# The second product of a mixture-of-experts kernel with its weights stationary, and row blocks turned on VectorE

## The chip, the cores and the metric

One of the eight cores of a Trainium2 chip runs the whole program. The metric is the time of one execution on the device in microseconds (us). TensorE (PE in the profile) multiplies: a weight load (PEld) puts a stationary operand of up to 128x128 into the array, and a matmul streams the columns of the moving operand past it into a bank of PSUM. VectorE is DVE, ScalarE is ACT, GpSimd is POOL and issues the indirect DMAs, SyncE (SP) issues the others.

## The reference, cut to what matters

Three layers follow one another: an attention between 512 tokens and 32 state rows per head, a dense layer with two products, and a mixture of eight experts.

```python
# attention: x [8, 8, 512, 64], state [8, 8, 32, 64]; rows read from the state, and state rows read from x
xread = softmax(x @ state.T / 8) @ state
sread = softmax(state @ x.T / 8) @ x
x = concat([xread, sread], axis=2)            # -> 4352 tokens x 512 after the heads are put side by side

# dense layer: w_in [512, 2048], w_out [2048, 512]
h = x @ w_in
g = h * clip(h + 3, 0, 6) / 6
x = g @ w_out                                  # the second product

# experts: w1 [8, 512, 1024], w2 [8, 1024, 512]
logits = x @ w_gate
e = argmax(logits)
gate = softmax(logits)[e] * sigmoid(x @ w_output_gate)[e]
out = gate * (relu(x @ w1[e]) @ w2[e])
```

## The kernel before

All products with high accuracy are made of three matmuls in the fp32r type: an operand is split into a high part (`gh`, `woh`, `sh`, `ah`) and a rest (`gl`, `wol`, `sl`, `al`), and high x high, high x rest and rest x high are added in one bank.

The dense layer is worked through in batches of 512 tokens (b = 0 to 7), and at the end the 256 state tokens (b = NB). A batch has 16 slices ft of the hidden dimension. For each, `h_xread` (state tokens: `h_sread`) makes a bank h of 128 hidden values by all tokens, `act` makes g, gh and gl from it on ACT and DVE in four instructions, and two slices later (LAG = 2) `second` calls `gemm2` for it. `gemm2` takes one token tile of 128 after another: gh and gl of the tile are stationary, the slice of w_out moves, and the bank `po[t]` collects 128 tokens by 512 model values over the 16 slices. The batches go in the order 0 (first half of the slices), 1, 0 (second half), 2 to 7, state tokens; the half results of batch 0 are kept in DRAM meanwhile (`half0`) and come back as `part`.

When a batch is through, `routed` scales its four banks by 1/6 into four row tiles `xr` of 513 values (ACT and DVE in turn; batch 0 on DVE, which adds `part`). During the next batch a timetable by slice number does the rest: steps 2 and 3 turn the rows (`turn_rows`: four TensorE transposes for a token tile into a bank, then a DVE copy to x2T), steps 6 to 8 multiply by the gate weights (`logits`, `turn_logits`), steps 9 to 11 choose the expert (`choose`), count the places (`ranks`) and, in `place`, make the gate weight, write it behind the row as its 513th value, and send the row tile to `xd` in DRAM; `scatter` writes the token numbers to a table `tab` at the tokens' places. A run of such TensorE instructions stays together (`one_run`) and waits before its first one for all that it needs. Batch 1 has a shorter timetable (`half_timetable`), batch 7 and the state tokens are routed between other instructions (`route`, `at_will`).

The experts are then run in slots of 256 places: `gather` reads token numbers out of `tab` and with them rows out of `xd`; `turn` turns the rows with TensorE and copies the gate weight out of the 513th value with POOL; `gemm1` and `gemm2e` are the products; `finish` scales by the gate and scatters rows to the output.

SP issues its DMAs in the order of the program: loads of the next batch (xT at step 2, xq at step 3), row writes at step 11. A tile's tag names a ring of buffers of which `bufs` exist; a writer waits until an earlier user of the buffer is done. The row tiles have the tag "xr" with four buffers of 2 KB; x2T lies in "x2T" (one) and for the second half of a batch in the ring "x4" of the loaded inputs.

Of the kernel before, what the change touches and what calls it, by code (L numbers as in the profile page):

```python
# [26 lines left out]
ROW = DM + 1  # L27
# [20 lines left out]
def cat_consts():  # L48
# [25 lines left out]
    tok = np.zeros((128, NT // 128), np.uint32)  # L74
    tok[:] = np.arange(NT).reshape(-1, 128).T
    fill = (NT + np.arange(NTAB).reshape(-1, 2) % 128).astype(np.uint32)
# [4 lines left out]
def tile_kernel(  # L81
# [32 lines left out]

    xd = tc.dram_tile([NT + 128, ROW], F32, name="xd")
    tab = tc.dram_tile([NTAB // 2, 2], U32, name="tab")
    half0 = tc.dram_tile([128, 4, DM], F32, name="half0")
    flat = tab.rearrange("a (b o) -> (a b) o", o=1)
# [15 lines left out]
    toku = cp.tile([128, NT // 128], U32, name="toku")  # L134
# [96 lines left out]
    def attn_rows_first(b):  # L231
# [6 lines left out]
        bt = ap.tile([128, 32, NS], F32, tag="t4", name="bt", bufs=2)  # L238
# [39 lines left out]
        with soon(b):  # L278
            af = ap.tile([128, 2, 512], F32, tag="t4", name="af", bufs=2)
            ah, al = [ap.tile([128, 2, 512], R32, tag=t, name=f"{t}{b}") for t in ("ah", "al")]  # L280
            flat2 = [t.rearrange("p a n -> p (a n)") for t in (bt, af)]
            V.tensor_tensor(bt, bt, sm[:, 8:40].unsqueeze(2).to_broadcast([128, 32, NS]), op=ALU.mult)
            V.transpose(flat2[1], flat2[0])
            S.copy(ah, af)
        yield
        with soon(b):
            V.tensor_tensor(al, af, ah.bitcast(F32), op=ALU.subtract)
# [3 lines left out]
    def attn_rows(b):  # L291
# [6 lines left out]
        bt = ap.tile([128, 32, NS], F32, tag="t4", name="bt", bufs=2)  # L298
# [27 lines left out]
        with soon0(b):  # L326
            V.tensor_tensor(bt, bt, rr.unsqueeze(2).to_broadcast([128, 32, NS]), op=ALU.mult)
            af = ap.tile([128, 2, 512], F32, tag="t4", name="af", bufs=2)
            ah, al = [ap.tile([128, 2, 512], R32, tag=t, name=f"{t}{b}") for t in ("ah", "al")]
            flat2 = [t.rearrange("p a n -> p (a n)") for t in (bt, af)]  # L330
            V.transpose(flat2[1], flat2[0])
            S.copy(ah, af)
        yield
        with soon0(b):
            V.tensor_tensor(al, af, ah.bitcast(F32), op=ALU.subtract)
# [172 lines left out]
    def routed(po, tile0, part=None):  # L508
        r = Route()
        r.tile0, r.nt = tile0, len(po)  # L510
        r.lg = mp.tile([128, 4, 32], F32, tag="lg", name="lg", bufs=1)[:, :r.nt, :]
        r.rows, r.made, r.x2, r.copies = [], [], {}, []
        for t in range(r.nt):
            xr = mp.tile([128, ROW], F32, tag="xr", name="xr", bufs=4)
            if part is not None:
                i = V.scalar_tensor_tensor(xr[:, :DM], po[t], 1.0 / 6.0, part[t // 2][:, t % 2, :], op0=ALU.mult,
                                           op1=ALU.add)
            elif t % 2:
                i = V.tensor_scalar(xr[:, :DM], po[t], 1.0 / 6.0, None, op0=ALU.mult)
            else:  # L520
                i = S.activation(xr[:, :DM], po[t], AF.Copy, scale=1.0 / 6.0)
            r.rows.append(xr)
            r.made.append(i.ins)
        return r

    def turn_rows(r, ts, home=None):

        def part():
            made = [misc() for _ in ts]
            for t in ts:  # L530
                if t % 2 == 0:
                    r.x2[t // 2] = (home or mp).tile([128, 4, 256], F32, tag="x4" if home else "x2T", name="x2T",
                                                     bufs=4 if home else 1)

            def use():
                for t, (ps, done) in zip(ts, made):
                    done.append(V.tensor_copy(r.x2[t // 2][:, :, 128 * (t % 2):128 * (t % 2) + 128],
                                              ps.rearrange("p (k t) -> p k t", k=4)).ins)
                    r.copies.append(done[-1])

            return [lambda t=t, k=k, ps=ps: T.transpose(ps[:, 128 * k:128 * k + 128],  # L541
                                                        r.rows[t][:, 128 * k:128 * k + 128], ident)
                    for t, (ps, _) in zip(ts, made) for k in range(4)], [r.made[t] for t in ts], use

        return part

    def logits(r, t0, n):

        def part():
            psl, done = misc()  # L550

            def mm(k, i):
                return T.matmul(psl[32 * k:32 * k + 32, 256 * i:256 * i + 256], wg_sb[:, k, :],
                                r.x2[t0 // 2 + i][:, k, :], start=True, stop=True, tile_position=(0, 32 * k))

            def use():
                r.l4 = mp.tile([128, 128 * n], F32, tag="x2T", name="l4", bufs=1)
                done.append(S.copy(r.l4, psl[:, :128 * n]).ins)
                r.l4_made = done[-1]

            return [lambda k=k, i=i: mm(k, i) for i in range(n // 2) for k in range(4)], list(r.copies), use
# [3 lines left out]
    def turn_logits(r, t0, n):  # L565

        def part():
            pst, done = misc()

            def use():  # L570
                done.append(V.tensor_reduce(r.lg[:, t0:t0 + n, :],
                                            pst[:, :128 * n].rearrange("p (t k c) -> p t c k", t=n, k=4),
# [3 lines left out]
                    for t in range(n)], [r.l4_made], use  # L576
# [46 lines left out]
    def place(r):  # L623

        nt, tile0, rows, z, ssum, psp = r.nt, r.tile0, r.rows, r.z, r.ssum, r.psp
# [15 lines left out]
        r.dsti = small(r, "ldsti", None, U32)  # L641
        V.tensor_copy(r.dsti, dst)  # L642

    def scatter(r, behind=()):

        new = []
        for t in range(r.nt):
            i = G.indirect_dma_start(flat, bass.IndirectOffsetOnAxis(ap=r.dsti[:, t:t + 1], axis=0),  # L648
                                     toku[:, r.tile0 + t:r.tile0 + t + 1], None).ins
# [21 lines left out]


    def from_f64(src, dst=None, sign=False, home=None):
# [7 lines left out]
        if dst is None:  # L681
            out = mp.tile([128, 512], F32, tag="xr", name="wz", bufs=4)
# [41 lines left out]
    def scratch():  # L724
        return mp.tile([128, 512], F32, tag="x2T", name="scr", bufs=1)
# [37 lines left out]
    left, used1, used2 = [one(t, NE) for t in ("left", "used1", "used2")]  # L763
    num, start = [one(t, 2 * NE) for t in ("num", "start")]
# [86 lines left out]
    def gather(n, table, idx, rows):  # L851

        ids = cp.tile([128, 2], U32, tag="ids", name="ids", bufs=6)
        i = G.indirect_dma_start(ids[:, :n], None, table, bass.IndirectOffsetOnAxis(ap=idx, axis=0)).ins
        after(i, placed)
        xg = []
        for t in range(n):
            x = qa["p"].tile([128, ROW], F32, tag="xg", name="xg", bufs=4) if qa else \
                mp.tile([128, ROW], F32, tag="xr", name="xg0", bufs=4)
            G.indirect_dma_start(x, None, rows, bass.IndirectOffsetOnAxis(ap=ids[:, t:t + 1], axis=0))  # L860
# [3 lines left out]
    def turn(xg):  # L864

        n = len(xg)
        gw = cp.tile([128, 2], F32, tag="gw", name="gw", bufs=4)
# [5 lines left out]
        for t in range(n):  # L873
# [3 lines left out]
            G.tensor_copy(gw[:, t:t + 1], xg[t][:, DM:DM + 1])  # L877
# [7 lines left out]
        return xh, xl, gw  # L885
# [64 lines left out]
    def finish(py, ids, gw, rows, quick=False):  # L950
        new = []
        for t in range(len(py)):
            y = mp.tile([128, DM], F32, tag="xr", name="y", bufs=4)
            if quick and t:
                V.tensor_scalar(y, py[t], gw[:, t:t + 1], None, op0=ALU.mult)
            else:
                S.activation(y, py[t], AF.Copy, scale=gw[:, t:t + 1])
            i = G.indirect_dma_start(rows, bass.IndirectOffsetOnAxis(ap=ids[:, t:t + 1], axis=0), y, None).ins
# [27 lines left out]
    def more_start():  # L986
# [3 lines left out]
        trow = mp.tile([128, ROW], F32, tag="x2T", name="trow", bufs=1)  # L990
# [11 lines left out]
    def second(n):  # L1002

        while len(held) > n:
            b, ft, gh, gl = held.pop(0)
            if b not in po_t:
                po_t[b] = [psum(f"o{t}") for t in range(gh.shape[1] // 128)]
            spill = b == 0 and ft == HALF - 1
            gemm2(po_t[b], ft, gh, gl, ft == 0 or (b == 0 and ft == HALF), ft == 15 or spill)
            if spill:  # L1010
                for t, p in enumerate(po_t.pop(b)):
                    xr = mp.tile([128, ROW], F32, tag="xr", name="xp", bufs=4)[:, :DM]
# [5 lines left out]
            if ft == 15:  # L1018
                later.append(routed(po_t.pop(b), 4 * b, part if b == 0 else None))
# [60 lines left out]
    def timetable(b, r, att):  # L1080
# [7 lines left out]
        at(2, lambda: one_run(turn_rows(r, [0, 1])))  # L1088
        at(3, lambda: one_run(turn_rows(r, [2, 3], ap)))
# [232 lines left out]
```

## Time and profile before

| | |
|---|---|
| median of 3 runs | 1136.89 us (1136.74 to 1137.72) |
| the profiled execution | 1139.82 us |
| its span, first to last instruction | 1138.0 us |
[...]
| busy: TensorE, VectorE, ScalarE, POOL | 97%, 62%, 49%, 12% of the span |
| DMA, mean over the span | 113 GB/s |

The stretches of the span: up to about 75 us weights are loaded and converted, up to 652 us the batches 0 to 7 run, up to 706 us the state tokens, and then the experts. Matmuls are pipelined and overlap, so the duration of one (0.39 us for 512 columns) is longer than the step from one to the next; what a matmul costs on TensorE is read from the steps between starts in the timeline, or from the pieces of the chain.

### The profile page before, as it was taken

Reading aid. Unit: us, or ns where it says so; the run is one execution under the profiler, and the core shown is the slowest. Engines: PE = TensorE matmul, PEld = TensorE weight load, DVE = VectorE, ACT = ScalarE, POOL = GpSimd, SP = SyncE. Lnnn points to the kernel's source line nnn. Section 1 sums busy time; section 2 is a strip of 40 time slices with the busy share of each in tenths; the row PEclk is TensorE's granted clock in tenths of the full one; section 3 lists DMA queues with packets and bytes.
Section 4 is the critical chain, followed back from the end, with each engine's and each line's share of the span. In section 5 each row is a group of like instructions: output and inputs, shape, how many; then the busy total and the mean of one; then the engine's idle time right before and its main releaser. Section 6 shows DMA issues by size and latency. Waiting matters only on the chain.

```text
span 1138.0 us, 18621 instructions
## 1 busy us (share of the span) xinstructions
PE 1102.1 (97%) x7008; PEld 873.1 (77%) x7008; DVE 703.2 (62%) x1457; ACT 556.6 (49%) x1062; POOL 134.7 (12%) x172
## 2 busy tenths in 40 slices
PE   3899999999999999999999999999999999999997
PEld 1557776777777777777777788889869986999994
DVE  6897857764655746747544476976546644666651
ACT  3778833433433433433333345556546554666651
POOL 0000000110010010010100113342122212222101
PEclk9999999999999999999999999999999999999999
DMA  8834012440130121300100019386175769822400
GB/s 270 294 115 145 21 47 65 87 86 1 56 58 1 57 58 37 78 1 19 38 1 28 10 38 263 109 317 242 44 263 195 248 214 318 320 83 92 141 20 30
DMA packets 54463, 128.32 MB, mean 113 GB/s; under 512 B 6736, under 2 KB 25424, under 8 KB 54352
## 3 DMA queue, kind: packets, MB, share of 16 engines
q1 hardware_dynamic: 47072, 108.66, 30.0%
q0 software_dynamic: 7296, 18.41, 4.6%
q8 instruction: 57, 0.93, 0.4%
q14 instruction: 38, 0.31, 0.1%
HBM read 136.98 MB, written 19.57 MB: 138 GB/s over the span
## 4 chain that ended last, share of the span: by engine, by line
PE 90%; DMA 4%; DVE 2%; issue 1%; ACT 1%; SPq 0%; POOL 0%; POOLq 0%; ACTq 0%; DVEq 0%
PE h L455 16%; PE h L925 16%; PE o L493 10%; PE o L495 10%; PE o L494 10%; PE o L941 5%; PE o L945 5%; PE o L944 5%; PE misc L223 4%; PE h L892 1%; PE misc L541 1%; PE misc L876 1%; PE o L911 1%; DMA w2s<-w 1%; DMA wi<-w_in 1%
## 5 line engine op out<-in xcount | busy, mean ns | idle before, releaser
L493 PE MATMUL o<-wo,gh 128*128 128x512 f32 x512 | 199.2, 393 | 1.7 <-ACT wo L708 1.7
L494 PE MATMUL o<-wo,gh 128*128 128x512 f32 x512 | 200.5, 392 | 0.0
L495 PE MATMUL o<-wo,gl 128*128 128x512 f32 x512 | 200.4, 391 | 0.0
L484 ACT ACTIVATE r<-h 128x512 f32<-128x512 f32 x128 | 76.6, 598 | 182.7 <-PE h L455 182.5
L485 DVE SCALAR_TENSOR_TENSOR g<-r,h 128x512 f32<-128x512 f32 x128 | 87.6, 684 | 117.3 <-ACT r L484 116.7
L931 DVE TENSOR_TENSOR vl<-w2s,vh 128x512 fp32r<-128x512 f32 x128 | 88.6, 692 | 104.8 <-ACT vh L930 83.9
L930 ACT CAST vh<-w2s 128x512 fp32r<-128x512 f32 x128 | 79.4, 620 | 99.8 <-PE o L945 95.0
L487 DVE TENSOR_TENSOR gl<-g,gh 128x512 fp32r<-128x512 f32 x128 | 88.3, 690 | 50.6 <-ACT gh L486 49.9
L493 PEld LDWEIGHTS o<-wo,gh 128*128 128x128 f32 x512 | 95.8, 188 | 28.8 <-issue 5.2
L455 PE MATMUL h<-ah,sh 128*128 128x512 f32 x256 | 108.0, 423 | 7.0 <-ACT sh L442 4.1
L486 ACT CAST gh<-g 128x512 fp32r<-128x512 f32 x128 | 79.2, 619 | 71.7 <-DVE g L485 70.9
L495 PEld LDWEIGHTS o<-wo,gl 128*128 128x128 f32 x512 | 96.3, 188 | 22.4 <-issue 1.8
L494 PEld LDWEIGHTS o<-wo,gh 128*128 128x128 f32 x512 | 96.4, 188 | 21.1 <-DVE wo L709 1.0
L648 POOL DMA_INDIRECT tab<-toku,ldsti x34 | 33.9, 997 | 651.7 <-DVE ldsti L642 392.9
L921 DVE TENSOR_TENSOR wl<-w1s,wh 128x512 fp32r<-128x512 f32 x128 | 88.8, 694 | 30.3 <-ACT wh L920 22.4
L455 PE MATMUL h<-al,sh 128*128 128x512 f32 x256 | 102.5, 401 | 0.0
L455 PE MATMUL h<-ah,sl 128*128 128x512 f32 x256 | 100.9, 395 | 0.0
L945 PE MATMUL o<-vh,hl 128*128 128x512 f32 x256 | 100.4, 392 | 0.0
L944 PE MATMUL o<-vl,hh 128*128 128x512 f32 x256 | 100.1, 391 | 0.0
L920 ACT CAST wh<-w1s 128x512 fp32r<-128x512 f32 x128 | 79.4, 622 | 38.9 <-PE h L925 33.2
L925 PEld LDWEIGHTS h<-xh,wh 128*128 128x128 f32 x512 | 76.5, 188 | 11.5 <-issue 1.6
L925 PE MATMUL h<-xh,wh 128*128 128x256 f32 x512 | 82.8, 283 | 1.1 <-ACT xh L881 1.1
(223 smaller groups left out, 1815.9 us busy)
## 6 DMA issues: line engine op xcount, KB each, us to landing
w1s<-w SPq DMA_DIRECT2D x88, 512.0 KB
w2s<-w SPq DMA_DIRECT2D x88, 512.0 KB
xd<-xr SPq DMA_DIRECT2D x34, 256.5 KB
xT<-xT SPq DMA_DIRECT2D x16, 512.0 KB
wi<-w_in SPq DMA_DIRECT2D x16, 512.0 KB
wraw<-w_out SPq DMA_DIRECT2D x16, 512.0 KB
xq<-xq SPq DMA_DIRECT2D x16, 512.0 KB
half<-xp SPq DMA_DIRECT2D x4, 256.0 KB
```

The costliest lines, as they stand in the source:

```text
L455: T.matmul(ps, w[:, o:o + 128], a[:, e, :], start=(n == 0), stop=(n == 5))
L485: V.scalar_tensor_tensor(g6, r, 6.0, ps, op0=ALU.min, op1=ALU.mult)
L487: V.tensor_tensor(gl, g6, gh.bitcast(F32), op=ALU.subtract)
L493: T.matmul(po[t], gh[:, s], woh[ft], start=first, stop=False)
L494: T.matmul(po[t], gh[:, s], wol[ft], start=False, stop=False)
L495: T.matmul(po[t], gl[:, s], woh[ft], start=False, stop=last)
L920: S.copy(wh, a)
L921: V.tensor_tensor(wl, a, wh.bitcast(F32), op=ALU.subtract)
L925: T.matmul(ps, w[:, k, :], x[:, k, :], start=(m == 0), stop=(m == 11))
L931: V.tensor_tensor(vl, c, vh.bitcast(F32), op=ALU.subtract)
L944: T.matmul(py[t], hh[:, sl], vl, start=False, stop=False)
L945: T.matmul(py[t], hl[:, sl], vh, start=False, stop=(ft == 7))
```

## The change

The second product is turned round: the slice of w_out, in four pieces of 128 model values, is stationary, and gh and gl of all tokens move. Each of the four banks then holds 128 model values by all tokens of the batch (512, or 256 state tokens). `routed` scales the banks into x2 with model values on the partitions, which is the form that `logits` reads, so `turn_rows` and its copies are gone. The rows for DRAM are made by VectorE: `write_rows` transposes 32x32 blocks of x2, 128x256 at a time, four to a tile `xr` for 256 tokens, at steps 2 and 3, and sends the tile in four DMAs of 32 partitions, whose pieces are 128 values (512 B). Within a row the model values thereby lie in another order, and w1 is laid out on the host to match. The gate weight no longer goes with the row but with the token's number: `toku` and `tab` hold pairs of number and gate, `gather` fetches pairs, and `finish` takes the gate from there; rows have 512 values, and the POOL copy in `turn` is gone.

Buffers: xr becomes a ring of two of 4 KB, also for outputs, gathered first rows and spilled halves. x2's first half lies in "x2T", the second in a new "x2b"; for batch 7 (tile0 == 28) the second lies in a buffer of the ring xr. Four tags of the attention become one ring "a4" of five; the staging of w_out goes to four fixed pieces in x2T and x2b; l4 goes to the ring "r".

The core of the diff, with what repeats left out:

```diff
     def gemm2(po, ft, gh, gl, first, last):
-        for t in range(len(po)):
-            s = slice(128 * t, 128 * t + 128)
-            T.matmul(po[t], gh[:, s], woh[ft], start=first, stop=False)
-            T.matmul(po[t], gh[:, s], wol[ft], start=False, stop=False)
-            T.matmul(po[t], gl[:, s], woh[ft], start=False, stop=last)
+        n = gh.shape[1]
+        for k in range(4):
+            s = slice(128 * k, 128 * k + 128)
+            T.matmul(po[k][:, :n], woh[ft][:, s], gh, start=first, stop=False)
+            T.matmul(po[k][:, :n], wol[ft][:, s], gh, start=False, stop=False)
+            T.matmul(po[k][:, :n], woh[ft][:, s], gl, start=False, stop=last)
...
-    def routed(po, tile0, part=None):
+    def routed(po, n, tile0, part=None):
...
-            xr = mp.tile([128, ROW], F32, tag="xr", name="xr", bufs=4)
+        x2 = [mp.tile([128, 1024 // n, n], F32, tag="x2T", name="x2T", bufs=1)]
+        if n == 512:
+            x2.append(mp.tile([128, 2, n], F32, tag="xr", name="x2b", bufs=2) if tile0 == 28 else
+                      ap.tile([128, 2, n], F32, tag="x2b", name="x2b", bufs=1))
+        r.x2 = [t[:, k, :] for t in x2 for k in range(1024 // n)]
+        r.made = []
+        for k in range(4):
+            dst, src = r.x2[k], po[k][:, :n]
...
-    def turn_rows(r, ts, home=None):
...
+    def write_rows(r, c):
+
+        xr = mp.tile([128, 8, 128], F32, tag="xr", name="xr", bufs=2)
+        for k in range(4):
+            i = V.transpose(xr[:, :, 32 * k:32 * k + 32], r.x2[k][:, 256 * c:256 * c + 256])
+            for d in r.made[1::2]:
+                tc.add_manual_dep(i.ins, d.name, LATER, reason="banks first")
+        r0 = 128 * r.tile0 + 256 * c
+        rows = xd[r0:r0 + 256, :].rearrange("(a u) (g n) -> g u a n", u=32, g=4)
+        for g in range(4):
+            D.dma_start(rows[g], xr[32 * g:32 * g + 32])
+
-    def logits(r, t0, n):
+    def logits(r):
...
-                return T.matmul(psl[32 * k:32 * k + 32, 256 * i:256 * i + 256], wg_sb[:, k, :],
-                                r.x2[t0 // 2 + i][:, k, :], start=True, stop=True, tile_position=(0, 32 * k))
+                return T.matmul(psl[32 * k:32 * k + 32, :r.n], wg_sb[:, k, :], r.x2[k], start=True, stop=True,
+                                tile_position=(0, 32 * k))
...
-        gw = small(r, "lgw")
-        V.reciprocal(gw, z)
-        for t in range(nt):
-            V.tensor_copy(rows[t][:, DM:DM + 1], gw[:, t:t + 1])
-            r0 = 128 * (tile0 + t)
-            D.dma_start(xd[r0:r0 + 128, :], rows[t])
+        V.reciprocal(toku[:, tile0:tile0 + nt, 1].bitcast(F32), z)
...
     def route(r):
 
-        for t0 in range(0, r.nt, 2):
-            at_will(turn_rows(r, [t0]))
-            yield
-            at_will(turn_rows(r, [t0 + 1]), logits(r, t0, 2), turn_logits(r, t0, 2))
-            yield
+        at_will(logits(r))
+        write_rows(r, 0)
+        yield
+        at_will(turn_logits(r))
+        if r.n > 256:
+            write_rows(r, 1)
+        yield
         choose(r)
         ranks(r)
         yield
...
-            G.tensor_copy(gw[:, t:t + 1], xg[t][:, DM:DM + 1])
...
-            y = mp.tile([128, DM], F32, tag="xr", name="y", bufs=4)
+            y, gw = ys[:, t, :], ids[:, 2 * t + 1:2 * t + 2].bitcast(F32)
...
-        at(2, lambda: one_run(turn_rows(r, [0, 1])))
-        at(3, lambda: one_run(turn_rows(r, [2, 3], ap)))
+        at(2, lambda: write_rows(r, 0))
+        at(3, lambda: write_rows(r, 1))
...
-            2: [lambda: one_run(turn_rows(r, [0, 1]))],
-            3: [lambda: at_will(logits(r, 0, 2), turn_logits(r, 0, 2)), row],
-            4: [lambda: one_run(turn_rows(r, [2, 3])), row],
-            5: [lambda: at_will(logits(r, 2, 2), turn_logits(r, 2, 2)), lambda: choose(r), row],
+            2: [lambda: write_rows(r, 0)],
+            3: [lambda: write_rows(r, 1), row],
+            4: [lambda: one_run(logits(r)), row],
+            5: [lambda: one_run(turn_logits(r)), lambda: choose(r), row],
...
-    w1 = c(inputs["moe2_w1"].reshape(NE, 4, 128, 4, EF // 4).transpose(0, 2, 3, 1, 4)).reshape(NE * 128, 4 * EF)
+    w1 = inputs["moe2_w1"].reshape(NE, 4, 4, 32, 4, EF // 4).transpose(0, 1, 3, 4, 2, 5)
+    w1 = c(w1).reshape(NE * 128, 4 * EF)
```

## Rows read from the trace of the kernel before

**Rows 1.** The page's busy times: us, share of the span, instructions.
```profile
PE 1102.1 (97%) x7008; PEld 873.1 (77%) x7008; DVE 703.2 (62%) x1457; ACT 556.6 (49%) x1062; POOL 134.7 (12%) x172
```

**Rows 2.** The chain that ended last: shares by engine, then by line.
```profile
PE 90%; DMA 4%; DVE 2%; issue 1%; ACT 1%; SPq 0%; POOL 0%; POOLq 0%; ACTq 0%; DVEq 0%
PE h L455 16%; PE h L925 16%; PE o L493 10%; PE o L495 10%; PE o L494 10%; PE o L941 5%; PE o L945 5%; PE o L944 5%; PE misc L223 4%; PE h L892 1%; PE misc L541 1%; PE misc L876 1%; PE o L911 1%; DMA w2s<-w 1%; DMA wi<-w_in 1%
```

**Rows 3.** Stretches: us; busy PE, PEld, DVE, ACT, POOL; clock, DMA share, GB/s.
```profile
50.00:75.00 25.00, 21.33 (x122) 13.06 (x121) 23.95 (x39) 17.70 (x33) 0.00 (x0) 1.00 0.37 126
75.00:110.00 35.00, 35.00 (x235) 26.91 (x235) 27.06 (x52) 28.80 (x54) 0.00 (x0) 1.00 0.57 176
...
280.00:360.00 80.00, 80.00 (x491) 60.58 (x490) 47.40 (x96) 31.76 (x57) 3.82 (x4) 1.00 0.17 41
...
645.00:706.00 61.00, 61.00 (x383) 53.46 (x382) 39.45 (x119) 28.39 (x62) 11.90 (x20) 1.00 0.40 107
706.00:740.00 34.00, 32.90 (x226) 29.15 (x225) 29.80 (x117) 19.31 (x40) 9.50 (x14) 1.00 0.41 151
```

**Rows 4.** Timeline of PE around one block: start, duration (us), instruction.
```profile
282.46 1.03 PE L541 MATMUL misc<-ident,xr 128*128 128x128 f32 x8
283.25 0.48 PE L455 MATMUL h<-ah,sh 128*128 128x512 f32 x1
283.57 0.40 PE L455 MATMUL h<-al,sh 128*128 128x512 f32 x1
```

**Rows 5.** Groups by form: names, count | busy us, mean ns | idle before.
```profile
L537 DVE COPY x2T<-misc 128x512 f32<-128x512 f32 x34 | 22.0, 686 | 6.2 <-PE misc L541 5.6 <-PE o L945 0.6
...
L541 PE MATMUL misc<-ident,xr 128*128 128x128 f32 x136 | 17.8, 273 | 0.0
...
L553 PE MATMUL misc<-x2T,wg_sb 128*32 128x256 f32 x136 | 9.5, 383 | 0.0
```

**Rows 6.** Pieces of the chain, 640 to 680 us: start, duration (us), what.
```profile
639.90 1.36 PE h L455 x6
641.26 0.23 PE o L493
...
675.65 1.41 PE h L469 x12
...
678.42 1.41 PE h L469 x12
```

**Rows 7.** Groups by form: transposes that VectorE already makes.
```profile
L331 DVE STREAM_TRANSPOSE af<-bt 128x1024 f32<-128x1024 f32 x7 | 8.7, 1238 | 0.0
...
L254 DVE STREAM_TRANSPOSE bt<-o 128x256 f32<-128x256 f32 x4 | 1.6, 426 | 4.9 <-PE o L250 4.9
```

**Rows 8.** Instructions on xd: ns min/median/max; landing in us.
```profile
L633 SPq DMA_DIRECT2D xd<-xr x34: 319/385/1830, 187.2 to 721.3; - x34
...
DMA to landing us min/median/max: 3.4/4.2/7.2
```

**Rows 9.** DMA queues of the page: packets, MB, share of 16 engines.
```profile
q1 hardware_dynamic: 47072, 108.66, 30.0%
```

**Rows 10.** Timelines of DVE and PE at the end of batch 0.
```profile
190.17 0.69 DVE L516 SCALAR_TENSOR_TENSOR xr<-o,part 128x512 f32<-128x512 f32 x1 [1.87 <-DMA xd<-xr]
...
194.90 1.09 PE L223 MATMUL misc<-win,st 64*32 64x512 f32 x16 [1.41 <-DVE x1l L412]
196.71 0.50 PE L455 MATMUL h<-ah,sh 128*128 128x512 f32 x1 [0.71 <-ACT sh L442]
```

**Rows 11.** Timelines of DVE, POOL and PE in the state tokens' stretch.
```profile
669.02 0.42 DVE L571 TENSOR_REDUCE lg<-misc 128x64 f32<-128x256 f32 x1
...
675.60 0.16 DVE L642 CAST ldsti<-ldst 128x4 uint32<-128x4 f32 x1
...
690.79 0.97 POOL L854 DMA_INDIRECT ids<-tab,idu  x1 [9.95 <-DVE ghl L487]
...
705.95 1.23 PE L876 MATMUL misc<-ident,xg 128*128 128x128 f32 x8
```

More of the change, by code (lines that the diff above doesn't have):

```diff
@@ L26 @@
 NTAB = TR + 256
-ROW = DM + 1
 N1 = -(-(NX - NE * 255) // 256)
@@ L133, in tile_kernel @@
     ones = cp.tile([128, 128], B16, name="ones")
-    toku = cp.tile([128, NT // 128], U32, name="toku")
+    toku = cp.tile([128, NT // 128, 2], U32, name="toku")
+    left, used1, used2 = [cp.tile([128, NE], F32, name=t) for t in ("left", "used1", "used2")]
+    num, start = [cp.tile([128, 2 * NE], F32, name=t) for t in ("num", "start")]
     x1h = cp.tile([128, 4, 2 * 128], R32, name="x1h")
@@ L506, in tile_kernel @@
         pass
-    def routed(po, tile0, part=None):
+    def routed(po, n, tile0, part=None):
         r = Route()
-        r.tile0, r.nt = tile0, len(po)
+        r.tile0, r.nt, r.n = tile0, n // 128, n
         r.lg = mp.tile([128, 4, 32], F32, tag="lg", name="lg", bufs=1)[:, :r.nt, :]
-        r.rows, r.made, r.x2, r.copies = [], [], {}, []
-        for t in range(r.nt):
-            xr = mp.tile([128, ROW], F32, tag="xr", name="xr", bufs=4)
+        x2 = [mp.tile([128, 1024 // n, n], F32, tag="x2T", name="x2T", bufs=1)]
[6 more added lines that the diff above has]
+            dst, src = r.x2[k], po[k][:, :n]
@@ L515, in routed @@
             if part is not None:
[L516 to L519, printed above, removed]
-            else:
-                i = S.activation(xr[:, :DM], po[t], AF.Copy, scale=1.0 / 6.0)
-            r.rows.append(xr)
+                i = V.scalar_tensor_tensor(dst, src, 1.0 / 6.0, part[k // 2][:, k % 2, :], op0=ALU.mult, op1=ALU.add)
+            elif k % 2:
+                i = V.tensor_scalar(dst, src, 1.0 / 6.0, None, op0=ALU.mult)
+            else:
+                i = S.activation(dst, src, AF.Copy, scale=1.0 / 6.0)
@@ L523, in routed @@
             r.made.append(i.ins)
         return r
-    def turn_rows(r, ts, home=None):
[L528 to L545, printed above, removed]
@@ L556, in use @@
             def use():
-                r.l4 = mp.tile([128, 128 * n], F32, tag="x2T", name="l4", bufs=1)
-                done.append(S.copy(r.l4, psl[:, :128 * n]).ins)
+                r.l4 = mp.tile([128, 512], F32, tag="r", name="l4")[:, :r.n]
+                done.append(S.copy(r.l4, psl[:, :r.n]).ins)
                 r.l4_made = done[-1]
-            return [lambda k=k, i=i: mm(k, i) for i in range(n // 2) for k in range(4)], list(r.copies), use
+            return [lambda k=k: mm(k) for k in range(4)], list(r.made), use
@@ L570, in use @@
             def use():
-                done.append(V.tensor_reduce(r.lg[:, t0:t0 + n, :],
-                                            pst[:, :128 * n].rearrange("p (t k c) -> p t c k", t=n, k=4),
+                done.append(V.tensor_reduce(r.lg, pst[:, :r.n].rearrange("p (t k c) -> p t c k", t=r.nt, k=4),
                                             axis=AX.X, op=ALU.add).ins)
             return [lambda t=t: T.transpose(pst[:, 128 * t:128 * t + 128], r.l4[:, 128 * t:128 * t + 128], ident)
-                    for t in range(n)], [r.l4_made], use
+                    for t in range(r.nt)], [r.l4_made], use
         return part
@@ L681, in from_f64 @@
         if dst is None:
-            out = mp.tile([128, 512], F32, tag="xr", name="wz", bufs=4)
+            if not words:
+                for home, tag in ((mp, "x2T"), (ap, "x2b")):
+                    two = home.tile([128, 2, 512], F32, tag=tag, name="wz", bufs=1)
+                    words.extend(two[:, i, :] for i in range(2))
+            out = words[len(woh) % 4]
             dst = out.rearrange("p (k n) -> p k n", k=k)
@@ L1006, in second @@
             if b not in po_t:
-                po_t[b] = [psum(f"o{t}") for t in range(gh.shape[1] // 128)]
+                po_t[b] = [psum(f"o{k}") for k in range(4)]
             spill = b == 0 and ft == HALF - 1
@@ L1018, in second @@
             if ft == 15:
-                later.append(routed(po_t.pop(b), 4 * b, part if b == 0 else None))
+                later.append(routed(po_t.pop(b), gh.shape[1], 4 * b, part if b == 0 else None))
     def step(gens):
@@ L1209, in drain @@
                 ids, _ = got.pop(s)
-                finish(py, ids, turned.pop(s)[2], out[0:NX, :] if ORDER[s][0] == "1" else out, s + 1 == first)
+                turned.pop(s)
+                finish(py, ids, out[0:NX, :] if ORDER[s][0] == "1" else out, s + 1 == first)
     banks = [2]
@@ L1222, in slot @@
                 turned[s] = turn(got[s][1])
-            xh, xl, _ = turned[s]
+            xh, xl = turned[s]
             args = gemm1(g % 2, ft, xh, xl)
@@ L1246, in pair @@
             turned[s] = turn(got[s][1])
-        x, _, gw = turned.pop(s)
+        x, _ = turned.pop(s)
         ps = psum("h", 2)
@@ L1266, in pair @@
             pair2(py, ft, hT[ft // 4])
-        finish([py], got.pop(s)[0], gw, out)
+        finish([py], got.pop(s)[0], out)
         if j + 1 < NP and j + 1 != CUT:
```

78 lines of the change are left out of this document (41 added, 37 removed).

## The prediction

> **What bounds the kernel now.** I read the page from the top. The busy times come first [rows 1]: TensorE (PE) is busy 1102.1 of 1138.0 us, VectorE (DVE) 62%, ScalarE (ACT) 49%. The chain of work that ended last says the same in another way [rows 2]: 90% of it is TensorE, and the two products and the expert products make nearly all of that; L541, the transposes that the change takes out, is 1.3% of the chain (14.8 us), L553, the logits, does not show. Shares over a whole span mix stages, so the busy times by stretch are next [rows 3]. In the middle of the program TensorE is busy 80.00 of 80 us while VectorE has 32.60 us free; the same holds in the stretch where the state tokens are worked on (645 to 706 us) and for all but 1.10 us of the 34 behind it, where VectorE is at 88%. Only the first stretch shown, where weights are converted, has VectorE at 96% and TensorE waiting 3.67 us of 25. So from about 75 us on, an instruction that leaves TensorE's queue shortens the program by its step in that queue, as long as no wait takes its place. The working below is about those two things.
>
> **The transposes that go.** The timeline of TensorE shows one block of eight (two token tiles) between a product and the next [rows 4]. The block starts at 282.46, the product behind it at 283.25 and its second matmul at 283.57. Matmuls of a product otherwise step at 0.23 us [rows 6], so without the block the second one would start at 282.46 + 0.23 = 282.69: the block costs 0.88 us, of which 0.79 are its own and the rest is for starting the product again. The group has 136 transposes [rows 5], 17 blocks of eight (the last as two of four): 17 x 0.88 = 14.96 us. Bounds: 17 x 0.79 = 13.4 if only the block's own time comes back, and 17.8, the busy time of the group, as the most.
>
> **The product turned round.** For 512 tokens the count is the same, 12 matmuls of 512 columns for each of the 16 slices of the hidden dimension; what was loaded as weights now moves, and the other way round. I take zero: the first product already has a converted weight (sh) as the loaded operand and 512 token columns moving, and takes 1.36 us for six [rows 6], which is 0.227 each, the step of the second product. For the 256 state tokens the count doubles and the columns halve: 6 x 0.227 = 1.36 us become 12 of 256 columns, for which the row of the state tokens' first product (12 in 1.41 us [rows 6]) gives 1.41; 16 x 0.05 = +0.8 us. A gain is excluded, as the columns are the same; the most is 0.02 us for each of the 192 short matmuls, 4 us, were their step to rise by a fifth.
>
> **The logits** move the same columns (512 as one matmul in place of two of 256), 9.5 us busy in all [rows 5]; I take zero. They now need the four scaled results instead of the copies of the transposed rows, which are made earlier.
>
> **Work on VectorE.** Out go 34 copies of 0.686 us (22.0 us [rows 5]) and 34 one-column copies of the gate. In come 68 transposes of 128x256 from SBUF. The trace has 128x256 from PSUM at 426 ns and 128x1024 from SBUF at 1238 ns [rows 7]; per element the longer one is cheaper (1.21 against 1.66 ns), so 68 of them cost between 68 x 0.310 = 21 and 68 x 0.426 = 29 us; I take the upper, whose shape is the same. For a batch that is 3.4 us where 2.7 go. It lies beside TensorE's work: 32.60 us of 80 are free. Cover gone, +0.7 us a batch on the path, 5.6 in all. [...]
>
> **Queues that the rows are moved past.** Row writes go from step 11 of a batch (place) to steps 2 and 3, ahead of the gate and of the load of xq on SP. Eight issues at 0.385 us each, the median row [rows 8], make 3.1 us on SP in a batch of about 77 us; behind them on SP stand the two xq loads, read at step 7, some 20 us later: hidden. The issues wait for VectorE's transposes, which wait only for the scaled results. POOL loses its gate copies, each of which waited for gathered rows; the chain has 0% of POOL [rows 2]. Packets: 4352 rows in four of 512 B make 13,056 more. A packet of queue q1 takes 0.30 x 16 x 1138 / 47072 = 0.116 us of one engine at 2.3 KB [rows 9]; at that price, an upper one, 13,056 x 0.116 / 16 = 95 us more in about 500 us, where the DMA share is 0.17 [rows 3]: no bound.
>
> **The stall at 194 us.** At the end of batch 0 the evacuations wait for row buffers still being written to DRAM: SP issues the writes from 187.2 on [rows 8], VectorE's first evacuation starts at 190.17 after 1.87 us "<-DMA xd<-xr", a copy behind it releases TensorE only at 194.90, after 1.41 us idle, and 0.71 more go before 196.71 [rows 10]. After the change the results go to x2T and x2b, free once batch 1's logits and transposes are through (steps 2 to 4 of six). The 1.41 go; the 0.71 behind them wait for ACT's half of the next operand and stay. -1.4 us, between 0 and -2.1.
>
> **The state tokens' stretch.** The chain there: logits of batch 7 read at 669.02, its places at 675.60, list entries fetched at 690.79, gathered rows transposed at 705.95 [rows 11], just when TensorE is done with the products. If it stayed put, what TensorE gains in this stretch would be lost: two blocks, 1.8 us. But it starts with the logits, which no longer wait for four transposes in two rounds, so it moves by more than TensorE does. I take zero.
>
> **Sum.** -14.96 + 0.8 - 1.4 = -15.6 us. The profiled execution ran 1139.82 us (span 1138.0 and 1.8 around it); the median of the runs is 1136.89, and the terms are taken from it: 1136.9 - 15.6 = 1121.3, said as 1121.
>
> **Rivals.**
> 1. *A wait on the row buffers eats part.* Batch 7 has its second half of x2 in one of the two row buffers, so its second four transposes need the buffer that the first four DMAs are still reading. VectorE works in order: behind them stand the state tokens' evacuations and batch 7's choice of experts. The DMAs on xd land in 3.4 to 7.2 us [rows 8]. The second product runs two slices behind the first, and a slice of the state tokens takes 678.42 - 675.65 = 2.77 us [rows 6], so TensorE has some 5.5 us of work in hand. Loss 0 to 7 us, the most if nothing of it is used: 1121 to 1128. Against it: a scheduler that puts other work first. Chance 0.14.
> 2. *Slower than before.* The same place, with a landing far longer. A half is 1024 packets of 512 B; at 0.116 us over 16 engines they take 7.4 us, and 4.2 to land: 12 us, less the 5.5 in hand a loss of 6, which rival 1 holds. But each DMA reads only 32 partitions; were it served by four engines, 29.7 + 4.2 = 34 us, less 5.5: 28 lost, 1149 us. It decides from a landing of about 21 us, where the loss is the whole gain. For it: nothing in the trace writes from so few partitions. Against: it happens once; the other batches have a buffer free for over 30 us. Chance 0.04.
> 3. *The same with half the engines:* 14.8 + 4.2 - 5.5 = 13.5 us lost, 1135, no change that can be told. Chance 0.03. [...]
> 4. *The product is slower with the operands exchanged.* Each of its 1536 matmuls of 512 columns need be only 10 ns slower to eat the gain (15 us): about 1137. For it: no row has just this pair. Against: [rows 6], the same kinds of operands at the same step. Chance 0.03.
> 5. *More than forecast:* the idle time that the sum leaves goes too (0.7 at the end of batch 0, 1.1 behind 706 us) and the group's whole 17.8 comes back: 15.6 + 0.7 + 1.1 + 2.8 = 20.2 less, 1116.7. Chance 0.04.
>
> **How the numbers follow.** Forecast (1117 to 1124) 0.72. The range takes in rivals 1 and 5: 1116 to 1128; about 1 in 10 is left out. Measurement tells about 0.2% (2.3 us) from no change: below 1134.6 counts as faster. Faster 0.90 (forecast, rivals 1 and 5), same 0.06 (rivals 3 and 4), slower 0.04 (rival 2).
>
> **What would show it.** Right: no transposes out of xr on TensorE, 136 fewer; products still at 0.23 us with wo loaded; TensorE busy 80 of 80 in the middle; batch length about 1.8 us shorter; the 1.41 us before the halves at the end of batch 0 gone. Wrong: a product step over 0.23; TensorE idle behind "DMA xd<-xr" near the state tokens' start; VectorE's transposes over 0.43 us, or gl late behind them so that products wait.

## The result and the profile after

| | before | after |
|---|---|---|
| median of the runs | 1136.82 us (1135.66 to 1137.72) | 1121.14 us (1120.30 to 1122.33) |
| profiled execution / its span | 1139.82 / 1138.0 us | 1122.33 / 1120.2 us |
| its mean granted clock of TensorE, as a share of full speed | 0.997 | 0.998 |

After over before: 0.9861, 95% interval 0.9848 to 0.9874, which is 15.8 us less (14.3 to 17.3). The prediction was 1121, between 1116 and 1128.

The page of the changed kernel: busy times, the chain by engine and by line, and queue q1.

```profile
PE 1087.2 (97%) x6904; PEld 862.6 (77%) x6904; DVE 699.4 (62%) x1456; ACT 556.5 (50%) x1061; POOL 125.6 (11%) x137
...
PE 93%; DVE 2%; DMA 1%; issue 1%; ACT 1%; SPq 0%; POOL 0%; POOLq 0%; DVEq 0%; ACTq 0%
PE h L459 16%; PE h L922 16%; PE o L498 11%; PE o L500 11%; PE o L499 11%; PE o L938 5%; PE o L942 5%; PE o L941 5%; PE misc L225 4%; PE h L473 2%; PE h L889 1%; PE misc L874 1%; PE o L908 1%; DMA wi<-w_in 1%; PE misc L552 1%
...
q1 hardware_dynamic: 60672, 108.80, 29.6%
```

TensorE has 14.9 us less to do than in [rows 1], the span is 17.8 us shorter, and TensorE is a larger share of the chain than in [rows 2]. VectorE is as busy as before. Queue q1 has 13,600 packets more than in [rows 9] and a smaller share of its engines' time.

Busy times by stretch of the changed kernel: us; busy PE, PEld, DVE, ACT, POOL; clock, DMA share, GB/s.

```profile
50.00:75.00 25.00, 21.34 (x120) 12.84 (x121) 24.69 (x41) 18.12 (x34) 0.00 (x0) 1.00 0.34 118
75.00:110.00 35.00, 35.00 (x236) 26.93 (x235) 27.42 (x53) 29.45 (x56) 0.00 (x0) 1.00 0.59 186
280.00:360.00 80.00, 80.00 (x476) 60.32 (x475) 47.04 (x96) 31.85 (x58) 3.84 (x4) 1.00 0.15 41
630.00:690.00 60.00, 59.97 (x447) 55.81 (x447) 37.94 (x117) 27.30 (x61) 14.69 (x21) 1.00 0.51 172
690.00:724.00 34.00, 33.15 (x227) 29.48 (x226) 31.75 (x122) 20.86 (x44) 9.01 (x8) 1.00 0.24 72
```

The bound has not moved [rows 3]: TensorE is nearly full from 75 us on, VectorE keeps 33 us free of 80 in the middle. Behind the state tokens' product TensorE loses 0.85 of 34 us where it lost 1.10.

Groups by form of the changed kernel, first TensorE's, then VectorE's: count | busy us, mean ns | idle before.

```profile
L500 PE MATMUL o<-gl,wo 128*128 128x512 f32 x512 | 200.2, 391 | 0.0
L498 PE MATMUL o<-ghl,wo 128*128 128x256 f32 x64 | 18.1, 283 | 0.0
```

```profile
L538 DVE STREAM_TRANSPOSE xr<-x2T 128x256 f32<-128x256 f32 x36 | 13.5, 412 | 0.0
L538 DVE STREAM_TRANSPOSE xr<-x2b 128x256 f32<-128x256 f32 x32 | 11.8, 407 | 0.0
```

L541 [rows 5] is gone from TensorE. In its place VectorE has 68 transposes, 25.3 us, within the 21 to 29 of the prediction.

**Where the time went.** ScalarE starts a relu (L484, after: L488) once for every slice of the hidden dimension, 144 times, always in the same order, so its starts are marks along both programs. Starts in us (slices 8 to 23 are batch 1, 24 to 31 the rest of batch 0, then 16 for each batch, and from 128 the state tokens); the last two columns are two of the experiments below.

| slice | before | after | before less after | blocks_back | gate_alone |
|---|---|---|---|---|---|
| 8 | 76.17 | 75.53 | 0.64 | 73.72 | 74.74 |
| 24 | 147.77 | 147.12 | 0.65 | 145.34 | 146.36 |
| 36 | 212.44 | 206.58 | 5.86 | 208.51 | 209.99 |
| 116 | 600.16 | 584.66 | 15.50 | 595.50 | 597.15 |
| 132 | 671.61 | 655.10 | 16.51 | 667.09 | 668.58 |
| 143 | 702.12 | 686.44 | 15.68 | 698.43 | 699.23 |
| span | 1138.0 | 1120.2 | 17.8 | 1133.1 | 1134.2 |

Slices 24 to 36 hold the blocks of batches 1 and 0 and the stall: 5.21 us. Slices 36 to 116 hold ten blocks: 9.64. Among the state tokens 0.83 is given back between 132 and 143.

### The profile page after: what moved, and what is told of

Read it like the earlier page. It is cut to its first block, busy times and chain, and to the rows that moved or that the text cites. A ratio compares the mean times of both kernels' runs of the same rounds, so it can differ in the third digit from the quotient of the medians.

```text
span 1120.2 us, 18393 instructions
## 1 busy us (share of the span) xinstructions
PE 1087.2 (97%) x6904; PEld 862.6 (77%) x6904; DVE 699.4 (62%) x1456; ACT 556.5 (50%) x1061; POOL 125.6 (11%) x137
## 4 chain that ended last, share of the span: by engine, by line
PE 93%; DVE 2%; DMA 1%; issue 1%; ACT 1%; SPq 0%; POOL 0%; POOLq 0%; DVEq 0%; ACTq 0%
PE h L459 16%; PE h L922 16%; PE o L498 11%; PE o L500 11%; PE o L499 11%; PE o L938 5%; PE o L942 5%; PE o L941 5%; PE misc L225 4%; PE h L473 2%; PE h L889 1%; PE misc L874 1%; PE o L908 1%; DMA wi<-w_in 1%; PE misc L552 1%
## 5 line engine op out<-in xcount | busy, mean ns | idle before, releaser
L499 PE MATMUL o<-gh,wo 128*128 128x512 f32 x512 | 200.1, 391 | 0.4 <-DVE wo L710 0.4
L498 PE MATMUL o<-gh,wo 128*128 128x512 f32 x512 | 198.9, 393 | 1.5 <-ACT wo L709 1.5
L500 PE MATMUL o<-gl,wo 128*128 128x512 f32 x512 | 200.2, 391 | 0.0
L488 ACT ACTIVATE r<-h 128x512 f32<-128x512 f32 x128 | 76.5, 598 | 167.4 <-PE h L459 167.4
L498 PEld LDWEIGHTS o<-gh,wo 128*128 128x128 f32 x512 | 96.1, 188 | 27.7 <-issue 4.4
L499 PEld LDWEIGHTS o<-gh,wo 128*128 128x128 f32 x512 | 96.1, 188 | 22.6 <-DVE wo L710 1.7
L500 PEld LDWEIGHTS o<-gl,wo 128*128 128x128 f32 x512 | 96.2, 188 | 21.4 <-issue 1.0
```

Source lines behind the costliest of these rows:

```text
L498: T.matmul(po[k][:, :n], woh[ft][:, s], gh, start=first, stop=False)
L499: T.matmul(po[k][:, :n], wol[ft][:, s], gh, start=False, stop=False)
L500: T.matmul(po[k][:, :n], woh[ft][:, s], gl, start=False, stop=last)
```

## The experiments

All are edits of the changed kernel; "before" was run beside each.

**blocks_back: the blocks alone.**

```diff
+    def blocks(r, ts):
...
+            return [lambda t=t, k=k, ps=ps: T.transpose(ps[:, 128 * k:128 * k + 128],
+                                                        r.x2[k][:, 128 * t:128 * t + 128], ident)
+                    for t, (ps, _) in zip(ts, made) for k in range(4)], list(r.made), lambda: None
...
-        at(2, lambda: write_rows(r, 0))
-        at(3, lambda: write_rows(r, 1))
+        at(2, lambda: write_rows(r, 0), lambda: one_run(blocks(r, [0, 1])))
+        at(3, lambda: write_rows(r, 1), lambda: one_run(blocks(r, [2, 3])))
```

> The changed kernel with the 17 blocks of eight TensorE transposes put back at the places where they stood before (steps 2 and 3 of a batch, and among the state tokens), into free PSUM banks and read by nobody; VectorE, the row writes, the product and the gate stay as changed. If the gain is the blocks' time in TensorE's queue: 17 x 0.88 = 15.0 us more than the changed kernel (13.4 to 17.8), about 1136. If the gain came from elsewhere (row buffers, queues, VectorE, the product turned round): 3 us more at most, below 1125.

Measured: 1135.44 us, 0.9996 of before (0.9987 to 1.0005). That is 14.3 us above the changed kernel by the medians, 15.3 by the two ratios. Timeline of its TensorE around one block:

```profile
278.44 0.38 PE L550 MATMUL misc<-ident,x2T 128*128 128x128 f32 x2
278.66 0.38 PE L550 MATMUL misc<-ident,x2b 128*128 128x128 f32 x2
278.88 0.38 PE L550 MATMUL misc<-ident,x2T 128*128 128x128 f32 x2
279.10 0.38 PE L550 MATMUL misc<-ident,x2b 128*128 128x128 f32 x2
279.23 0.48 PE L459 MATMUL h<-ah,sh 128*128 128x512 f32 x1
279.55 0.40 PE L459 MATMUL h<-al,sh 128*128 128x512 f32 x1
```

From 278.44 to 279.23 and 279.55, to the hundredth the spacing of [rows 4]: the block costs 0.88 us whether or not VectorE copies it out. By the table it is (595.50 - 208.51) - (584.66 - 206.58) = 8.91 us for the ten blocks between slices 36 and 116, 0.89 each, of the 9.64 that the change brings there. The gain is the blocks.

**gate_alone: the change with the product, the blocks and their copies as before.**

```diff
-            T.matmul(po[k][:, :n], woh[ft][:, s], gh, start=first, stop=False)
+            T.matmul(po[t], gh[:, s], woh[ft], start=first, stop=False)
...
+        for t in (2 * c, 2 * c + 1):          # write_rows: rows as they lie, 128 partitions
+            D.dma_start(xd[r0:r0 + 128, :], r.rows[t])
...
+        at(2, lambda: write_rows(r, 0), lambda: one_run(turn_rows(r, [0, 1])))
```

> The changed kernel with the product, the TensorE transposes and their copies as before, and w1's rows in their old order: what is left of the change is that the gate goes with the token's number and that rows are written at once, 128 partitions of 2 KB each. Theory: only the 1.41 us at the end of batch 0 go, so 1.4 less than before (0 to 2.1), about 1135. Rival: early rows and the gate carry a good part of the gain, 5 us less than before or more, 1132 or below.

Measured: 1135.95 us, 0.9995 of before (0.9986 to 1.0004), so 0.6 us less, with 0.5 more and 1.6 less as the ends. The rival (5 us or more) falls. The timeline of its TensorE at the end of batch 0 shows where the small gain lies:

```profile
191.74 0.40 PE L499 MATMUL o<-wo,gl 128*128 128x512 f32 x1
192.52 1.09 PE L225 MATMUL misc<-win,st 64*32 64x512 f32 x16 [0.38 <-DVE x1l L416]
194.33 0.50 PE L459 MATMUL h<-ah,sh 128*128 128x512 f32 x1 [0.71 <-ACT sh L446]
```

Of the 1.41 us ahead of L223 in [rows 10] 0.38 are left. From slice 36 to 116 it takes 387.16 us, blocks_back 386.99: the product with its operands as before, its copies and its other row writes make 0.17 us in five batches. The kernel before takes 387.72 there, so 0.56 us came with the gate and the early rows.

**turns_twice and turns_six: what hides VectorE's transposes.**

```diff
-            i = V.transpose(xr[:, :, 32 * k:32 * k + 32], r.x2[k][:, 256 * c:256 * c + 256])
+            for _ in range(2):      # turns_six: range(6)
+                i = V.transpose(xr[:, :, 32 * k:32 * k + 32], r.x2[k][:, 256 * c:256 * c + 256])
```

> The changed kernel with each of VectorE's 68 transposes done twice into the same place: 68 x 0.405 = 27.5 us more on VectorE. Theory: hidden beside TensorE, within 1 us of the changed kernel, 1120 to 1122.5. Rival: VectorE's work around steps 2 and 3 makes gl late, so that the products wait: 1.6 us a batch and 0.8 of the state tokens, up to 14 us more, 1135; with no cover at all 27.5 more, 1149.

> The changed kernel with each of VectorE's transposes done six times into the same place: 5 x 27.3 = 137 us more on VectorE, 16 us in each batch of some 75, in which it has some 30 free. If it is the share of free time that hides them: 0 to 1 more, 1122. If it is the order in VectorE's queue: the 48 transposes of a batch (19 us) come in one stretch of about seven slices of 4.1 us, and where more than some 5 us of them stand ahead of a g or gl the products wait: 2 to 5 us a batch, 1137 to 1161.

Measured: twice 1121.93 us, 0.9869 of before (0.9854 to 0.9885), the changed kernel's time within the intervals; six times 1155.04 us, 1.0162 of before (1.0145 to 1.0179), 33.9 us more than the changed kernel. The busy times of 280 to 360 us with two of each:

```profile
280.00:360.00 80.00, 80.00 (x476) 60.34 (x475) 49.42 (x104) 32.40 (x58) 3.84 (x4) 1.00 0.18 48
```

VectorE has 2.4 us more than the changed kernel there, and TensorE stays at 80.00. With six of each VectorE still has 21.55 us free in the same stretch (58.45 busy), but TensorE is busy for only 78.73. The timeline of turns_six, VectorE and then TensorE, shows why:

```profile
296.88 3.34 DVE L539 STREAM_TRANSPOSE xr<-x2T 128x256 f32<-128x256 f32 x10
300.14 0.41 DVE L539 STREAM_TRANSPOSE xr<-x2b 128x256 f32<-128x256 f32 x1
300.47 0.41 DVE L539 STREAM_TRANSPOSE xr<-x2T 128x256 f32<-128x256 f32 x1
300.80 3.35 DVE L539 STREAM_TRANSPOSE xr<-x2b 128x256 f32<-128x256 f32 x10
304.06 0.65 DVE L489 SCALAR_TENSOR_TENSOR g<-r,h 128x512 f32<-128x512 f32 x1
```

```profile
304.77 0.50 PE L459 MATMUL h<-ah,sh 128*128 128x512 f32 x1 [1.27 <-DVE g L489]
```

A run of 22 transposes, 7.2 us, stands ahead of a g, and TensorE waits 1.27 us for it. Free time in the stretch did not help: what counts is how much stands ahead of the next g against TensorE's work in hand. By slices 36 to 116 it is 6.0 us in five batches, 1.2 each, less than the 2 to 5 expected; of the 33.9 us 12.0 arise between slices 28 and 32, at the end of batch 0, and 14.7 from slice 116 on, around the state tokens and behind them.

Not all of this is waiting, and not all the waiting is for a g. At the end of batch 0 (165 to 210 us) TensorE waits 9.1 us, of which only 0.6 are for a g and 8.5 for other results; behind the longest, 3.2 us that the trace puts down to VectorE's lpos, the granted clock fell (busy times of turns_six):

```profile
195.00:200.00 5.00, 2.96 (x71) 2.19 (x68) 5.00 (x18) 1.59 (x4) 0.00 (x0) 0.56 0.00 0
200.00:205.00 5.00, 3.59 (x20) 1.61 (x21) 4.83 (x15) 1.07 (x2) 0.00 (x0) 0.50 0.20 38
205.00:210.00 5.00, 5.00 (x27) 2.73 (x25) 2.49 (x6) 1.70 (x3) 0.00 (x0) 0.58 0.20 44
```

By these rows some 5 us are lost to the clock (an estimate: busy time by what is missing to 1.00, 2.96 x 0.44 + 3.59 x 0.50 + 5.00 x 0.42). In all four executions of turns_six its mean was 0.987 to 0.990, in those of the changed kernel 0.997 to 0.999, so a part of the 33.9 us is lost to the clock behind the waits and not in them.

**one_buffer, forced_wait, forced_but_last: rivals 1 to 3 made to happen.**

```diff
-        xr = mp.tile([128, 8, 128], F32, tag="xr", name="xr", bufs=2)
+        if c == 0:
+            r.xr = mp.tile([128, 8, 128], F32, tag="xr", name="xr", bufs=2)
+        xr = r.xr
...
+        while ahead:    # not in one_buffer; in act: the next slice's g comes behind the second half
+            tc.add_manual_dep(i.ins, ahead.pop().name, LATER, reason="second half first")
```

In forced_wait and forced_but_last both halves are also written at step 2 and not at steps 2 and 3; forced_but_last leaves batch 7 out of the second edit.

> The changed kernel with one row buffer for both halves of a batch: in each of the eight batches (and not only where it could happen in batch 7) the second four transposes must wait until the first four writes have read the buffer. This prices rivals 1 to 3. If 16 DMA engines serve the writes, they land within 12 us at most and VectorE, or whoever stands behind in its queue, loses 0 to 6.5 us a batch: 1121 to 1173. Half the engines: 13.5 us a batch, 1229. Four engines: 28 us a batch, 1345. If the instructions behind the wait are put ahead of it by the order in which they are queued: 0, 1121.

> One row buffer for both halves of a batch, and VectorE's order fixed so that the second four transposes stand ahead of the next slice's g, some 3.3 us after the first of the four writes is issued instead of 7.3 (run one_buffer, where nobody waited: 272.34 to 279.66). VectorE should now be seen waiting for the writes: at most 4.0 us a batch, as in one_buffer the buffer was free within 7.3. If TensorE has two slices (some 5 us) in hand, nothing or little is lost: 1121 to 1124. If nothing is in hand, the whole wait is lost in each of eight batches: up to 32 us, 1153. No wait seen at all: the writes have read the buffer within 3.3 us of the first issue.

> As forced_wait, but batch 7's second half is left where it stands in the changed kernel; the other seven batches keep the fixed order and wait for their writes (7.3 us in all there). If the 4.6 us of forced_wait come only from batch 7's place, behind which the state tokens' rg stood: 0 to 1 more than the changed kernel, 1121 to 1122. If each wait costs a part of itself: up to 7 more, 1128.

Measured: one_buffer 1120.51 us, 0.9857 of before (0.9842 to 0.9872); forced_wait 1125.72, 0.9902 (0.9885 to 0.9918); forced_but_last 1121.12, 0.9866 (0.9849 to 0.9882). In one_buffer the order of VectorE's queue had the second four transposes 7.3 us behind the first write, and nobody waited. In forced_wait they do; its timeline of VectorE and then of SP, and the sum of the waits (us, times, longest):

```profile
276.14 0.69 DVE L495 TENSOR_TENSOR gl<-g,gh 128x512 fp32r<-128x512 f32 x1 [0.69 <-ACT gh L494]
277.92 0.77 DVE L544 STREAM_TRANSPOSE xr<-x2T 128x256 f32<-128x256 f32 x2 [1.08 <-DMA xd<-xr]
```

```profile
273.53 7.67 SPq L552 DMA_DIRECT2D xd<-xr  x8
```

```profile
DVE xr L544 <- DMA xd<-xr: 7.3, 7, 2.3
```

The first write is issued at 273.53 and all four have read the buffer by 277.92: 4.4 us. Seven waits, 7.3 us in all, and they cost nothing: TensorE is busy 100.00 of the 100 us from 260 on, and forced_but_last, which keeps the wait in seven batches, has the changed kernel's time. The 4.6 us come from batch 7, and there from no DMA: its second half, at 656.18, has no wait for one. Timeline of TensorE in forced_wait, then its busy times over four short stretches:

```profile
654.67 0.63 PE L473 MATMUL h<-x1h,wil 128*128 128x256 f32 x4
658.05 0.83 PE L473 MATMUL h<-x1h,wih 128*128 128x256 f32 x4 [2.76 <-DVE rg L491]
658.68 0.42 PE L502 MATMUL o<-ghl,wo 128*128 128x256 f32 x1
658.89 0.41 PE L503 MATMUL o<-ghl,wo 128*128 128x256 f32 x1
```

```profile
655.00:658.00 3.00, 0.29 (x3) 0.10 (x1) 2.42 (x7) 0.60 (x2) 2.39 (x3) 1.00 0.03 3
658.00:660.00 2.00, 1.95 (x11) 1.98 (x12) 1.82 (x8) 1.27 (x4) 1.33 (x2) 0.62 0.65 125
660.00:662.00 2.00, 2.00 (x11) 2.00 (x11) 1.71 (x12) 0.17 (x1) 0.00 (x0) 0.53 0.75 136
662.00:664.00 2.00, 2.00 (x19) 2.00 (x18) 0.85 (x3) 1.30 (x3) 0.00 (x0) 1.00 0.08 3
```

The state tokens' rg was held behind the second half, TensorE idled 2.76 us, and behind that the granted clock was 0.62 and then 0.53, for 2 us each: matmuls of 256 columns step at 0.21 us instead of 0.12. Some 1.7 us of those 4 are lost to it (an estimate from these rows: 2 x 0.38 + 2 x 0.47), which with the 2.76 makes 4.5 of the 4.6.

**rows_twice: the row writes' traffic.**

```diff
             D.dma_start(rows[g], xr[32 * g:32 * g + 32])
+        rows = xd2[r0:r0 + 256, :].rearrange("(a u) (g n) -> g u a n", u=32, g=4)
+        for g in range(4):
+            D.dma_start(rows[g], xr[32 * g:32 * g + 32])
```

> The changed kernel with every row written twice, the second time into a DRAM tensor that nobody reads: 68 more DMAs of 32 partitions, 17408 more packets of 512 B, 8.7 MB. Theory: queues and DMA engines have room, within 1 us of the changed kernel, 1120 to 1122.5. Rival: SP's issues (8 x 0.46 = 3.7 us more a batch) or the engines hold up the loads of xq and of the next batch, or the state tokens' gathers behind the last rows: 3 us or more, 1124 and up.

Measured: 1120.87 us, 0.9865 of before (0.9848 to 0.9881): no difference from the changed kernel. Neither SP's issues nor the DMA engines became a bound: from 260 to 360 us TensorE is busy for 100.00 of 100, at a DMA share of 0.25.

**cols_256: what shorter matmuls cost.**

```diff
-            T.matmul(po[k][:, :n], woh[ft][:, s], gh, start=first, stop=False)
+            for c in range(0, n, 256):
+                q = slice(c, c + 256)
+                T.matmul(po[k][:, q], woh[ft][:, s], gh[:, q], start=first and c == 0, stop=False)
...
```

> The changed kernel with every 512-column matmul of the second product cut into two of 256: 1536 matmuls become 3072, the columns stay. It prices what the change does to the state tokens alone. By the state tokens' rows (12 of 256 columns in 1.43 us, against 6 of 512 in 1.36) a slice of 512 tokens takes 24 of 256 in 2.86 against 2.72: 0.14 x 128 = 18 us more, about 1139. Rival: a cut costs only where weights change, and here two matmuls share none, so 24 weight loads in place of 12 stand in the way: 0.188 us busy each, which a matmul of 256 columns (0.117) can't cover: 24 x 0.19 = 4.5 us a slice, 128 x 1.8 = 230 more, 1350.

Measured: 1135.58 us, 0.9995 of before (0.9986 to 1.0005), 14.4 us above the changed kernel by the medians, 15.2 by the ratios. Timeline of its TensorE:

```profile
310.61 0.28 PE L500 MATMUL o<-gh,wo 128*128 128x256 f32 x1
...
313.36 0.28 PE L502 MATMUL o<-gl,wo 128*128 128x256 f32 x1
```

These are the first and the last of the 24 matmuls of a slice: 23 steps in 2.75 us, 0.120 each, where half of 0.227 would be 0.114. From slice 28 to 124 its relus fall back from the changed kernel's by 13.42 us, 0.14 a slice, as the rows priced it. From slice 8 to the end the traces differ by 16.8 us, 0.14 for each of 120 slices. What is missing to 18 us lies ahead of slice 8, which the profile of cols_256 reaches 3.60 us before that of the changed kernel (71.93 against 75.53); whether TensorE's waits for converted weights hide the cost there, or executions differ so at the start, is not shown. The rival (a weight load in the way of every matmul, 230 us) falls.

## Why the prediction held, step by step

- **The blocks, -14.96 (13.4 to 17.8).** Right. Put back alone they cost 14.3 to 15.3 us, 0.89 for each between slices 36 and 116. Not the whole busy time of the group (17.8) and not only its own 0.79: starting the product again counts, as 0.88 had it.
- **The product turned round, 0.** Right: L498 to L500 take 391 to 393 ns with wo loaded, as L493 to L495 did before, and the two experiments with either operand loaded differ by 0.17 us in five batches. Rival 4 asked for 10 ns a matmul.
- **State tokens, +0.8.** The mechanism was right, the size a little low: from slice 132 to 140 the relus take 22.83 us where they took 22.24, 0.074 a slice, 1.2 in 16. cols_256 shows the same step on the batches' product.
- **The logits, 0.** Right: from their first matmul to the next product it is 0.98 us before (309.26 to 310.24) and 0.97 after (301.46 to 302.43).
- **The stall at 194 us, -1.4 (0 to -2.1).** Right where it stands; timeline of VectorE and then TensorE in the changed kernel, against [rows 10]:

```profile
188.36 0.69 DVE L526 SCALAR_TENSOR_TENSOR x2T<-o,part 128x512 f32<-128x512 f32 x1 [3.72 <-PE o L500]
...
190.02 1.28 DVE L526 SCALAR_TENSOR_TENSOR x2b<-o,part 128x512 f32<-128x512 f32 x2
```

```profile
190.50 1.09 PE L225 MATMUL misc<-win,st 64*32 64x512 f32 x16
192.32 0.50 PE L459 MATMUL h<-ah,sh 128*128 128x512 f32 x1 [0.73 <-ACT sh L446]
```

  No evacuation waits for a DMA, L225 follows the product at once, and the 0.7 us behind it stayed, as said. Early rows alone (gate_alone) bring 1.03 of the 1.41; in its median that is too small to tell from nothing.
- **VectorE, hidden.** Right, with the price between the two rows: 0.407 to 0.412 us against the 0.426 taken, and the shorter operation dearer per element (1.6 ns for 128x256 against 1.21 for the 128x1024 of [rows 7]). But the reason given (32.60 us of 80 are free) is not the one that decides: in turns_six 21.55 us are free in that stretch and TensorE waits, 1.27 us for one g.
- **Queues and packets, 0.** Right: twice the writes change nothing (1120.87 us against 1121.14). The changed kernel's trace names no engine that waited for a DMA on xd, where before POOL's gate copies waited 77.6 us for gathered rows and VectorE 2.9 us for row buffers.
- **The state tokens' chain, 0.** Right. POOL's fetches and TensorE's turn of the gathered rows in the changed kernel:

```profile
665.74 0.97 POOL L853 DMA_INDIRECT ids<-tab,idu  x1 [4.99 <-DVE rg L489]
...
672.85 0.94 POOL L859 DMA_INDIRECT xg<-xd,ids  x1 [3.45 <-ACT wih L467]
```

```profile
690.49 1.04 PE L874 MATMUL misc<-ident,xg 128*128 128x128 f32 x8
692.34 0.73 PE L922 MATMUL h<-xh,wh 128*128 128x256 f32 x4 [0.81 <-ACT xh L878]
```

  The entries are fetched 25.0 us earlier than in [rows 11], where TensorE's turn comes 15.5 us earlier; the turn follows the product at once.
- **Rival 1, the wait on the row buffer.** It did not come, for the reason named against it: in the changed kernel batch 7's second half stands at 656.17, 10 us behind the first. forced_wait shows what the place is worth: its 4.6 us lie within the 0 to 7, but they come through rg in VectorE's queue and the clock behind it, not through the DMA, so that the price fits is luck.
- **Rivals 2 and 3, writes from 32 partitions.** Four of them have read their buffer 4.4 us after the first issue, where four engines would have needed 34 us and half of them 19 by the prediction's price. That price, 0.116 us a packet, was far too high: at it even 16 engines would need 7.4 + 4.2. While the first four of a batch run in the changed kernel, issued from 273.41 on with no other transfer in its timelines, the DMA share is 0.70, 0.94 and 0.91 of the 16 engines in the three us from 274 to 277, where four engines could make 0.25 and half of them 0.5. So the four together keep nearly all of them busy; what one such write alone would reach is not shown.
- **Not told apart.** The spans of the profiled executions differ by 17.8 us, their times by 17.5, the medians by 15.7. The profile of before was 3.0 us above its median, that of after 1.2; 0.64 of the difference arose before slice 8, where neither has come to a block or a row write. From slice 8 to the end the traces differ by 17.2 us, and 14.7 of these are what blocks_back gives back. By the same count gate_alone is 2.4 us shorter than before, 1.03 of it the stall; the rest (chiefly 0.56 between slices 36 and 116 and 0.91 behind slice 143) stands where the prediction had put nothing. Its median shows 0.6. The parts are known to about 1 us, so that their sum met the median within 0.2 us is in part luck.

## What to carry to other kernels

Where TensorE is full, an instruction taken from its queue is worth its step there plus the restart behind it, read off one timeline, times its count (here 0.79 and 0.09 us for a block of eight transposes, 0.89 measured when put back); the engine that takes the work over is free of charge as long as no more of it stands ahead of the next operand than TensorE has work in hand (here transposes done twice cost nothing that could be measured, and a run of 7.2 us ahead of a g cost 1.27). Look at that run in the queue, not at the share of free time in the stretch. In this product, which operand is loaded and which moves is no matter at 512 columns (391 to 393 ns a matmul either way); halving the columns costs some 5% (steps of 0.120 us, where half of 0.227 would be 0.114).

## What was not expected

**The clock behind a short wait.** One idle time of 2.76 us was followed by 4 us at a granted clock of 0.62 and 0.53 in forced_wait, and the waits of turns_six at the end of batch 0 by 15 us at 0.50 to 0.58, so a stall can cost more than itself (some 4.5 us for the 2.76, by the estimate above). A clock as low shows at the start. Busy times from 40 to 50 us, the changed kernel and then blocks_back, whose program is the same up to there:

```profile
40.00:50.00 10.00, 9.65 (x57) 5.64 (x58) 9.29 (x19) 6.12 (x14) 0.00 (x0) 0.83 0.70 251
```

```profile
40.00:50.00 10.00, 8.65 (x59) 4.67 (x57) 8.81 (x16) 7.55 (x16) 0.00 (x0) 1.00 0.87 307
```

The clock granted was 0.83 in the one (0.54 from 40 to 42 us, 0.61 from 42 to 44), behind 1.63 us in which TensorE waited for sh, and 1.00 in the other, whose slice 8 starts 1.81 us earlier (73.72 against 75.53). Whether such differences at the start make the 2 to 4 us by which executions of one kernel differ, no run here shows; the mean clock does not: in 21 executions of before those at 0.996, 0.997, 0.998 and 0.999 took 1136.9, 1136.6, 1136.6 and 1136.5 us on average.
